# Attention of batches 3 to 7 at other steps, and another order in the prologue, in an attention and mixture-of-experts kernel

## The chip, the core and the metric

The kernel runs on one core of one Trainium2 chip. The metric is the device time of one execution in microseconds (us). The core has five engines with a queue each: TensorE (PE; its weight loads are PEld), VectorE (DVE), ScalarE (ACT), GpSimd (POOL) and SyncE (SP), which here issues the DMAs.

## The reference

For each of 8 batches and 8 heads, 576 tokens with 64 features are first gathered into 32 memory slots by a softmax of phi, each token then attends to the slots, and the result, 4608 rows of 512, goes through four experts whose outputs are summed with the given probabilities:

```python
a = np.exp(phi - np.max(phi, axis=2, keepdims=True))
a = a / (np.sum(a, axis=2, keepdims=True) + 1e-09)
k_m = np.einsum('bhsm,bhsd->bhmd', a, k)
v_m = np.einsum('bhsm,bhsd->bhmd', a, v)
attn = softmax(1.0 / np.sqrt(64) * np.matmul(q, k_m.transpose(0, 1, 3, 2)))
x = rows_of(np.matmul(attn, v_m))            # 4608 x 512
p = domain_probs / (domain_probs.sum(-1, keepdims=True) + 1e-09)
for e in range(4):
    out += p[:, e:e + 1] * (np.maximum(x @ w1[e], 0.0) @ w2[e])
```

## The kernel before

**Numbers in two parts.** A float32 factor is held as a rounded part ("high", cast by ScalarE) and the remainder ("low", input minus high, by VectorE or GpSimd). A product takes three matmuls: high x high, high x low, low x high. So nearly every tile needs a cast and a subtraction: of weights in `split` (L142, L143), of keys and values in `kv_split` (L266, L267), of h in `first` (L565, L567).

**The steps.** Batches go in four pairs. x @ w1 is not formed through x: the attention weights of a batch (AT, transposed) are multiplied by vw, the product of v_m and w1. `first(s)` makes one 128-row block of h for a half of a batch (six matmuls of 256 or 320 columns, L553 to L555; L565 and L567 empty the bank), `second(s)` multiplies such a block with w2 (six or nine matmuls of 512 columns, L583 to L585), summing in PSUM over 8 steps, after which `accumulate` (L603, L605) weighs the sums by the expert's probability into acc. There are 512 steps: 128 per pair (PAIR), 32 per expert (STEPS), 16 per batch, 8 per half. One step runs `accumulate` when sums have ended, then the work that the plan holds for it, then `first(s + 2)` and `second(s)`.

**The products vw.** `vw_mm` multiplies v of two batches with a block of w1 (L453 to L455); `vw_out` (L473, L474) empties it: for each of the two batches a cast of 64x512 on ScalarE and a subtraction on VectorE, both from PSUM. For the pairs and experts that concern us `vw_steps` puts the matmuls at a step and the emptying into the next. Emptying stands in steps 51, 52, 59 to 64; 115, 116, 123 to 128; 147, 148, 155 to 160; 179, 180, 187 to 192.

**Attention in the plan.** The table ATT has a row for each of the batches 2 to 7: a start step, the steps of the scores' matmuls, and the steps of the transposes. `attention(b, s, scores, turns)` puts the parts at fixed distances from the start s: `load_phi` at s; the maxima `phi_max` (L192, two per batch) at s + 3; the exponentials `phi_exp` (L201) at s + 4; the norms `phi_norm` (L206 to L209) at s + 5 and s + 6; transposes of the weights (tpa, L223) and their emptying into a (L231, L232) from s + 7; for each of four head pairs hp a `kv_split` at s + 10 + 3 hp, matmuls (L278, into x) two steps later, their copy xs (`kv_out`, L289) one after that; `kv_fold` (kvp) at s + 18 and s + 24 with `kv_pick` (L311, L312) a step later; `v_hi` at s + 26 and `write_vs` (vs, L367 to L370) at s + 27. Scores are made by `scores_mm` and, in the three following steps, `scores_max` (L393, L396), `scores_exp` (L402) and `soft` (L409 to L412).

**PSUM.** Four banks ("pm") go round for h's sums, products, x, kvp, scores and transposes, and four ("p2") for the second product. A matmul that takes a bank waits until the last user's emptying is done.

**Order.** From step 36 (FREE) on, instructions run on each engine in the order of the program; before that a scheduler orders them, except for the prologue, written out by hand (L755 to L839): batch 0's attention, its four products, the first weights. `keep_warm` issues matmuls on an identity tile. Remainders of the first w1 block are made by GpSimd but for one by VectorE; the first w2 block is cast there by ScalarE, and its remainders made by VectorE in L836. Products 0 and 2 go through `vw_out_by_copy`: two ScalarE copies, and a GpSimd subtraction (L482) from the SBUF copy. Loads of inputs go into `stage` tiles (L128) and are issued in the order in which the plan takes them; a load waits for its buffer.

Of the kernel before, what the change touches and what calls it, by code (L numbers as in the profile page):

```python
# [31 lines left out]
F32 = mybir.dt.float32  # L32
F32R = mybir.dt.float32r
# [8 lines left out]
P = 128  # L42
# [10 lines left out]
STAGE = 4  # L53
# [19 lines left out]
PAIR_AT = ((18, 19, 26, 27), (28, 29, 30, 31))  # L73

ATT = {
    2: (22, (92, 96, 100), (97, 101, 104)),
    3: (42, (104, 107, 110), (112, 113, 114)),
    4: (PAIR, (PAIR + 40, PAIR + 44, PAIR + 48), (PAIR + 45, PAIR + 49, PAIR + 53)),
    5: (PAIR + 22, (PAIR + 76, PAIR + 80, PAIR + 84), (PAIR + 112, PAIR + 113, PAIR + 114)),
    6: (PAIR + 44, (2 * PAIR + 24, 2 * PAIR + 28, 2 * PAIR + 32), (2 * PAIR + 29, 2 * PAIR + 33, 2 * PAIR + 37)),  # L80
    7: (PAIR + 66, (2 * PAIR + 98, 2 * PAIR + 102, 2 * PAIR + 106), (2 * PAIR + 112, 2 * PAIR + 113, 2 * PAIR + 114)),
}

UNITS_1 = (1, 5, 5, 6, 5, 6, 8, 9, 10, 11, 11, 12, 17, 13, 13, 20)
# [7 lines left out]
def body(ctx: ExitStack, tc: tile.TileContext, qm, qt, kv, kvt, phi, prob, w1, w1d, w2, out):  # L92
# [16 lines left out]
        kind, *i = key  # L109
        return {"kv": kv, "kvt": kvt, "qm": qm, "qt": qt, "w1": w1, "w1d": w1d, "w2": w2}[kind][tuple(i)]  # L110

    order, staged, count = [], {}, [0, 0]

    def stage_ahead(upto):
        while count[0] < min(upto, len(order)):
            i, src = count[0], source(order[count[0]])
            if STAGE <= i < STAGE + 4:
                t = work.tile([P, 1024], F32, name="stage", tag="acc", bufs=4)
            else:
                t = work.tile([P, 1024], F32, name="stage", tag="stage", bufs=STAGE)  # L120
            n = 1
            for d in src.shape[1:]:
                n *= d
            names = "abcd"[:len(src.shape) - 1]
            t = t[:, :n].rearrange(
                f"p ({' '.join(names)}) -> p {' '.join(names)}", **dict(zip(names, src.shape[1:]))
            )
            nc.sync.dma_start(t, src)  # L128
            staged[i] = t
            count[0] += 1  # L130
# [170 lines left out]
    def kv_pick(b, g):  # L301
        if g == 0:
            st["v", b] = att.tile([P, NP, M], F32, name="v", tag="v", bufs=2)
        for w in range(2):
            for i in range(2):
                r, m = slice(64 * i, 64 * i + 64), slice(M * i, M * i + M)
                lo = slice(2 * M + M * i, 2 * M + M * i + M)
                a = slice(2 * g, 2 * g + 2)
                dst = st["v", b][r, a] if w else kT[b % 4][r, a, m]
                src = st["kvp", b, g][r, :, w]  # L310
                (nc.vector.tensor_copy if i and b == 0 else nc.scalar.copy)(dst, src[:, :, m])  # L311
                nc.vector.tensor_add(dst, dst, src[:, :, lo])  # L312

    def unit_kv(b, hp):
        def emit(raw):
# [157 lines left out]
            nc.scalar.copy(t[r, 0, :], ps[r])  # L473
            nc.vector.tensor_sub(t[r, 1, :], ps[r], t[r, 0, :].bitcast(F32))  # L474

    def vw_out_by_copy(ps, fh, hp):
        g, r = hp // 2, slice(64 * (hp % 2), 64 * (hp % 2) + 64)
        t = vw_tile(0, 0, 0, fh, g)
        tmp = att.tile([P, 2, 512], F32, name="vwc", tag="vw1", bufs=5)
        nc.scalar.copy(tmp[r, 0, :], ps[r])  # L480
        nc.scalar.copy(t[r, 0, :], ps[r])
        nc.gpsimd.tensor_sub(t[r, 1, :], tmp[r, 0, :], t[r, 0, :].bitcast(F32))  # L482
# [157 lines left out]
    for fh in range(2):  # L640
        for g in range(2):
            at(W1_1[2 * fh + g], unit_w1(0, 0, fh, g))
            for i in range(2):
                vw_at(VW_1[4 * fh + 2 * g + i], 0, 0, fh, 2 * g + i, (1,))
    def attention(b, s, scores, turns):

        at(s, lambda: load_phi(b))
        for g in range(2):
            at(s + 3, lambda g=g: phi_max(b, g))
            at(s + 4, lambda g=g: phi_exp(b, g))  # L650
            at(s + 5 + g, lambda g=g: phi_norm(b, g))
            at(s + 7 + g, lambda g=g: phi_turn(b, g))
            at(s + 8 + g, lambda g=g: phi_turn_out(b, g))
        at(s + 9, lambda: phi_turn_tail(b))
        at(s + 9, unit_tail(b))
        at(s + 10, lambda: phi_turn_tail_out(b))
        for hp in range(NP):
            def load(raw, hp=hp):
                for c2 in range(2):
                    kv_split(b, hp, raw, c2, nc.gpsimd)  # L660
            def multiply(hp=hp):
                for c2 in range(2):
                    kv_mm(b, hp, c2)
                kv_mm_tail(b, hp)
            at(s + 10 + 3 * hp, (("kv", b, hp), load))
            at(s + 12 + 3 * hp, multiply)
            at(s + 13 + 3 * hp, lambda hp=hp: kv_out(b, hp))
        for g in range(2):
            at(s + 18 + 6 * g, lambda g=g: [kv_fold(b, 2 * g + i) for i in range(2)])
            at(s + 19 + 6 * g, lambda g=g: kv_pick(b, g))  # L670
        def write():
            if b < 4:
                write_vt(b)
        at(s + 26, lambda: (v_hi(b), write()))
        at(s + 27, lambda: write_vs(b))
        for t0, n in zip((0, 2, 4), scores):
            at(n, (q_key(b, t0), lambda q, t0=t0: scores_mm(b, t0, q)))
            at(n + 1, lambda t0=t0: scores_max(b, t0))
            at(n + 2, lambda t0=t0: scores_exp(b, t0))
            at(n + 3, lambda t0=t0: soft(b, t0))  # L680
        for t0, n in zip((0, 2, 4), turns):
            at(n, lambda t0=t0: transposes(b, t0))
            at(n + 1, lambda t0=t0: transposes_out(b, t0))
# [72 lines left out]
    with tc.manual_schedule():  # L756
        raw = {key: take(later) for later, key in enumerate(early)}
        stage_ahead(len(early) + 4)
        nc.scalar.copy(att.tile([P, 1], F32, name="woken", tag="woken"), ident[:, :1])
        nc.sync.dma_start(pt, prob)  # L760
        keep_warm(10)
        dve, gps = nc.vector, nc.gpsimd
        for g in range(2):
            phi_max(0, g)
        for g in range(2):
            phi_exp(0, g)
        kvr = lambda hp: raw["kv", 0, hp]
# [24 lines left out]
        for hp in (2, 3):
            for c2 in range(2):
                kv_mm(0, hp, c2)
            kv_mm_tail(0, hp)
            if hp == 2:
                for i in range(2):
                    kv_fold(0, i)
        keep_warm(3)
        kv_pick(0, 0)  # L800
        w1g = [raw["w1", 0, 0, g] for g in range(2)]
        split_w1(w1g[0], 0, 0, gps)
        for hp in (2, 3):
            kv_out(0, hp)
        write_vt(0, slice(0, 1))
        q = raw["qm", 0, 0]
        scores_mm(0, 0, q, (0, 1))
        for hp in (2, 3):
            kv_fold(0, hp)
        keep_warm(5)  # L810
        kv_pick(0, 1)
        scores_mm(0, 0, q, (2, 3))
        split_w1(w1g[0], 0, 1, dve)
        write_vt(0, slice(1, 2))
        keep_warm(2)
        split_w1(w1g[1], 0, 2, gps)
        split_w1(w1g[1], 0, 3, gps)
        for i in range(2):
            t = wp.tile([P, 2, DM], F32R, name="w2", tag="w2", bufs=NJ + 1)
            nc.scalar.copy(t[:, 0, :], raw["w2", 0, 0][:, i, :])  # L820
            w2t[0, 0, i] = t
        scores_max(0, 0)
        scores_exp(0, 0)
        pv = [vw_mm(0, 0, hp, ("p2", 4)) for hp in range(4)]
        vw_out_by_copy(pv[0], 0, 0)
        vw_out_by_copy(pv[2], 0, 2)
        soft(0, 0)
        keep_warm(6)
        vw_out(pv[1], 0, 0, 0, 1, (0,))
        transposes(0, 0)  # L830
        transposes_out(0, 0)
        keep_warm(4)
        vw_out(pv[3], 0, 0, 0, 3, (0,))
        for i in range(2):
            t = w2t[0, 0, i]
            dve.tensor_sub(t[:, 1, :], raw["w2", 0, 0][:, i, :], t[:, 0, :].bitcast(F32))  # L836
        for s in range(AHEAD):
            first(s)
        probabilities()  # L839
# [53 lines left out]
```

## Time and profile before

| | us |
|---|---|
| median of three runs | 1423.62 (1422.99 to 1423.77) |
| the profiled execution | 1424.37 |
| its span, first to last instruction | 1422.6 |
| TensorE busy in the span | 1396.9 (98%) |
| VectorE busy | 653.1 (46%) |
| ScalarE busy | 568.6 (40%) |
| GpSimd busy | 395.3 (28%) |

The mean granted TensorE clock is 0.996 of full. A row of the timeline gives the start of an instruction in us from the span's start, its duration, the engine, the line, output <- input, and in brackets the idle time before it with what ended it. Matmul ends are modelled: the row of a matmul is longer than the distance to the next one. A row "xN" holds N instructions that follow one another.

### The profile page before, as it was taken

How to read it: one execution, taken by the hardware profiler on the slowest of the kernel's cores; microseconds unless marked ns; L12 is line 12 of the kernel's file. 1: busy time of each engine (PE TensorE's matmuls, PEld its weight loads, DVE VectorE, ACT ScalarE, POOL GpSimd, SP SyncE). 2: the span in 40 equal slices, each digit the busy share in tenths (PEclk: the TensorE clock that was granted, in tenths of full speed). 3: DMA queues.
4: the chain of work that ended last, by engine and by line, in shares of the span. 5: the costliest groups of instructions: out<-in, count | busy, mean ns of one | idle time of the engine just before them, and what ended most of it. 6: DMA issues, size and time to landing. Idle time of an engine off the chain costs nothing.

```text
span 1422.6 us, 21651 instructions
## 1 busy us (share of the span) xinstructions
PE 1396.9 (98%) x7748; PEld 1217.2 (86%) x7748; DVE 653.1 (46%) x1565; ACT 568.6 (40%) x1524; POOL 395.3 (28%) x315
## 2 busy tenths in 40 slices
PE   7999999999999989999999999999999999999998
PEld 7788888888888878888888888888888888888887
DVE  7885454535553546454443345434343322223222
ACT  7655455533354454553353443534332312122221
POOL 4300244412234162433342433424220202020200
PEclk9999999999999999999999999999999999999999
DMA  5632322684233143234468676786841623333201
GB/s 202 209 108 90 106 74 92 225 255 132 75 128 95 56 132 97 72 109 140 131 230 269 228 270 185 260 229 217 256 139 45 186 75 104 75 104 75 60 31 37
DMA packets 62843, 199.16 MB, mean 140 GB/s; under 512 B 10384, under 2 KB 11536, under 8 KB 62736
## 3 DMA queue, kind: packets, MB, share of 16 engines
q1 hardware_dynamic: 62736, 197.77, 44.4%
q8 instruction: 62, 1.02, 0.3%
q14 instruction: 45, 0.37, 0.1%
HBM read 146.35 MB, written 51.38 MB: 139 GB/s over the span
## 4 chain that ended last, share of the span: by engine, by line
PE 91%; DVE 4%; ACT 3%; DMA 1%; issue 1%; POOL 0%; SPq 0%; ACTq 0%; DVEq 0%
PE p L585 18%; PE p L584 17%; PE p L583 17%; PE p L553 9%; PE p L555 9%; PE p L554 9%; PE pv L506 3%; PE x L278 2%; PE sc L383 2%; DVE vw L474 1%; ACT vw L473 1%; ACT w L142 1%; PE tp L433 1%; PE pv L453 1%; DMA stage<-in_w 1%
## 5 line engine op out<-in xcount | busy, mean ns | idle before, releaser
L143 POOL TENSOR_TENSOR w<-stage,w 128x512 fp32r<-128x512 f32 x227 | 293.2, 1294 | 734.0 <-ACT w L142 710.4
L567 DVE SCALAR_TENSOR_TENSOR h<-p,h 128x256 fp32r<-128x256 f32 x512 | 215.5, 421 | 440.7 <-ACT h L565 303.0
L585 PE MATMUL p<-w,h 128*128 128x512 f32 x1024 | 402.7, 394 | 1.0 <-DVE nm L195 1.0
L584 PE MATMUL p<-w,h 128*128 128x512 f32 x1024 | 401.4, 392 | 0.4 <-DVE w L143 0.4
L583 PE MATMUL p<-w,h 128*128 128x512 f32 x1024 | 401.8, 393 | 0.0
L565 ACT ACTIVATE h<-p 128x256 fp32r<-128x256 f32 x512 | 196.6, 385 | 482.7 <-PE p L555 464.2
L553 PE MATMUL p<-AT,vw 128*128 128x256 f32 (+1 forms) x1024 | 307.8, 301 | 8.5 <-DVE vw L474 3.1
L555 PE MATMUL p<-AT,vw 128*128 128x256 f32 (+1 forms) x1024 | 302.5, 296 | 0.1
L554 PE MATMUL p<-AT,vw 128*128 128x256 f32 (+1 forms) x1024 | 301.8, 295 | 0.7 <-DVE AT L445 0.7
L585 PEld LDWEIGHTS p<-w,h 128*128 128x128 f32 x1024 | 192.3, 188 | 43.9 <-DVE nm L195 1.5
L553 PEld LDWEIGHTS p<-AT,vw 128*128 128x128 f32 x1024 | 192.7, 188 | 30.3 <-ACT xs L289 3.7
L584 PEld LDWEIGHTS p<-w,h 128*128 128x128 f32 x1024 | 192.5, 188 | 23.1 <-DVE w L143 0.8
L583 PEld LDWEIGHTS p<-w,h 128*128 128x128 f32 x1024 | 192.6, 188 | 22.6 <-ACT h L565 0.3
L554 PEld LDWEIGHTS p<-AT,vw 128*128 128x128 f32 x1024 | 192.8, 188 | 20.2 <-DVE AT L445 0.9
L555 PEld LDWEIGHTS p<-AT,vw 128*128 128x128 f32 x1024 | 192.4, 188 | 0.4 <-issue 0.3
L142 ACT CAST w<-stage 128x512 fp32r<-128x512 f32 x262 | 161.1, 618 | 7.3 <-DMA stage<-in_w 5.0
L567 DVE SCALAR_TENSOR_TENSOR hm<-p,hm 128x64 fp32r<-128x64 f32 x256 | 56.1, 219 | 139.0 <-ACT h L565 137.5
L565 ACT ACTIVATE hm<-p 128x64 fp32r<-128x64 f32 x256 | 57.0, 223 | 153.1 <-PE p L555 153.0
L509 DVE TENSOR_TENSOR vst<-pv,vst 128x512 fp32r<-128x512 f32 x80 | 55.3, 692 | 111.4 <-ACT vst L508 111.1
L267 POOL TENSOR_TENSOR kvs<-stage,kvs 128x512 fp32r<-128x512 f32 x58 | 75.0, 1314 | 98.9 <-ACT kvs L266 98.0
L508 ACT CAST vst<-pv 128x512 fp32r<-128x512 f32 x80 | 47.0, 587 | 121.9 <-PE pv L506 120.5
L474 DVE TENSOR_TENSOR vw<-pv,vw 64x512 fp32r<-64x512 f32 x94 | 64.4, 688 | 29.6 <-ACT vw L473 28.1
(95 smaller groups left out, 1174.0 us busy)
## 6 DMA issues: line engine op xcount, KB each, us to landing
stage<-in_w SPq DMA_DIRECT2D x92, 512.0 KB, 4.0
vwd<-vst SPq DMA_DIRECT2D x80, 512.0 KB, 3.5
vw<-vwd SPq DMA_DIRECT2D x320, 128.0 KB, 4.0
stage<-in_w1d SPq DMA_DIRECT2D x40, 512.0 KB, 3.8
stage<-in_kv SPq DMA_DIRECT2D x32, 512.0 KB, 3.8
stage<-in_qm SPq DMA_DIRECT2D x16, 512.0 KB, 4.2
out<-acc SPq DMA_DIRECT2D x32, 256.0 KB, 2.1
ph<-in_phi SPq DMA_DIRECT2D x16, 288.0 KB, 4.2
```

The source lines that it names most:

```text
L142: nc.scalar.copy(dst[:, 0, :], raw)
L143: eng.tensor_sub(dst[:, 1, :], raw, dst[:, 0, :].bitcast(F32))
L267: eng.tensor_sub(t[:, 1], src, t[:, 0].bitcast(F32))
L474: nc.vector.tensor_sub(t[r, 1, :], ps[r], t[r, 0, :].bitcast(F32))
L553: nc.tensor.matmul(ps, w[:, 0, f], at_t[:, g, 0, c], start=g == 0, stop=False)
L554: nc.tensor.matmul(ps, w[:, 0, f], at_t[:, g, 1, c], start=False, stop=False)
L555: nc.tensor.matmul(ps, w[:, 1, f], at_t[:, g, 0, c], start=False, stop=g == 1)
L565: nc.scalar.activation(t[:, 0, to], ps[:, at_], AF.Relu)
L567: nc.vector.scalar_tensor_tensor(t[:, 1, to], ps[:, at_], 0.0, t[:, 0, to].bitcast(F32), ALU.max, ALU.subtract)
L583: nc.tensor.matmul(po[t], x[:, 0, :], w[:, 0, :], start=j == 0, stop=False)
L584: nc.tensor.matmul(po[t], x[:, 0, :], w[:, 1, :], start=False, stop=False)
L585: nc.tensor.matmul(po[t], x[:, 1, :], w[:, 0, :], start=False, stop=j == NJ - 1)
```

## The change

ATT gets one more column, the step at which `v_hi` and `write_vs` stand (before: start + 26). Batch 2 stays. Batch 3 starts 4 steps earlier. Batch 4 keeps its start, is written 9 steps later, and its scores and transposes stand 6 to 8 steps earlier. Batch 5 starts 4 steps later, batches 6 and 7 start 4 steps earlier. `kv_pick` issues its four copies and then its four adds, where a copy and an add alternated. In the prologue `vw_out_by_copy` is gone: all four products are emptied by `vw_out`. GpSimd makes the remainder of one more w1 block and of both w2 blocks (now by `split_w2`), three `keep_warm` matmuls less are issued ahead of the transposes and four stand behind them instead of behind their emptying. Two more loads get a buffer of their own at the start, in a tile of the kind AT. Lines after the table shift by 5 to 10.

```diff
 ATT = {
-    3: (42, (104, 107, 110), (112, 113, 114)),
-    5: (PAIR + 22, (PAIR + 76, PAIR + 80, PAIR + 84), (PAIR + 112, PAIR + 113, PAIR + 114)),
+    3: (38, 65, (104, 107, 110), (112, 113, 114)),
+    5: (PAIR + 26, PAIR + 53, (PAIR + 76, PAIR + 80, PAIR + 84), (PAIR + 112, PAIR + 113, PAIR + 114)),
 ...
-            if STAGE <= i < STAGE + 4:
+            if STAGE + 4 <= i < STAGE + 6:
+                if i == STAGE + 4:
+                    spare.append(att.tile([P, 2 * 2 * S], F32, name="stage", tag="AT", bufs=3))
+                t = spare[0][:, 1024 * (i - STAGE - 4):1024 * (i - STAGE - 3)]
+            elif STAGE <= i < STAGE + 4:
 ...
-                (nc.vector.tensor_copy if i and b == 0 else nc.scalar.copy)(dst, src[:, :, m])
-                nc.vector.tensor_add(dst, dst, src[:, :, lo])
+                parts.append((dst, src[:, :, m], src[:, :, lo]))
+        for n, (dst, hi, _) in enumerate(parts):
+            (nc.vector.tensor_copy if n == 1 and b == 0 else nc.scalar.copy)(dst, hi)
+        for dst, _, lo in parts:
+            nc.vector.tensor_add(dst, dst, lo)
 ...
-        at(s + 26, lambda: (v_hi(b), write()))
-        at(s + 27, lambda: write_vs(b))
+        at(written, lambda: (v_hi(b), write()))
+        at(written + 1, lambda: write_vs(b))
 ...
-        split_w1(w1g[0], 0, 1, dve)
+        split_w1(w1g[0], 0, 1, gps)
 ...
-        for i in range(2):
-            t = wp.tile([P, 2, DM], F32R, name="w2", tag="w2", bufs=NJ + 1)
-            nc.scalar.copy(t[:, 0, :], raw["w2", 0, 0][:, i, :])
-            w2t[0, 0, i] = t
         scores_max(0, 0)
+        pv = [vw_mm(0, 0, hp, ("p2", 4)) for hp in range(4)]
+        vw_out(pv[0], 0, 0, 0, 0, (0,))
         scores_exp(0, 0)
-        pv = [vw_mm(0, 0, hp, ("p2", 4)) for hp in range(4)]
-        vw_out_by_copy(pv[0], 0, 0)
-        vw_out_by_copy(pv[2], 0, 2)
         soft(0, 0)
-        keep_warm(6)
-        vw_out(pv[1], 0, 0, 0, 1, (0,))
+        keep_warm(3)
+        for hp in (1, 2):
+            vw_out(pv[hp], 0, 0, 0, hp, (0,))
         transposes(0, 0)
+        keep_warm(4)
         transposes_out(0, 0)
-        keep_warm(4)
         vw_out(pv[3], 0, 0, 0, 3, (0,))
         for i in range(2):
-            t = w2t[0, 0, i]
-            dve.tensor_sub(t[:, 1, :], raw["w2", 0, 0][:, i, :], t[:, 0, :].bitcast(F32))
+            split_w2(0, 0, i, raw["w2", 0, 0], gps)
```

VectorE's queue at the end of the prologue, before, from the softmax sum of batch 0's first scores to h of step 0 (h_401). The numbers tell tiles apart; w1_458 and w1_461 are blocks of the next half of w1:

```order
L409 TENSOR_REDUCE z_363<-at_334 128x16
L410 TENSOR_SCALAR z_363<-z_363 128x16
L411 RECIPROCAL z_363<-z_363 128x16
L412 TENSOR_TENSOR at_334<-at_334,z_363 128x512
L474 TENSOR_TENSOR vw_353<-pv_341,vw_353 64x512
L143 TENSOR_TENSOR w1_458<-stage_115,w1_458 128x512
L445 TENSOR_TENSOR AT_377<-tp_378,AT_377 128x2x256
L474 TENSOR_TENSOR vw_358<-pv_349,vw_358 64x512
L836 TENSOR_TENSOR w2_328<-stage_111,w2_328 128x512
L836 TENSOR_TENSOR w2_330<-stage_111,w2_330 128x512
L567 SCALAR_TENSOR_TENSOR h_401<-p1_394,h_401 128x256
```

The same place after (h of step 0 is h_393, the blocks of the next half of w1 are w1_450, w1_453, w1_458):

```order
L148 TENSOR_TENSOR w1_450<-stage_114,w1_450 128x512
L418 TENSOR_REDUCE z_351<-at_329 128x16
L419 TENSOR_SCALAR z_351<-z_351 128x16
L420 RECIPROCAL z_351<-z_351 128x16
L421 TENSOR_TENSOR at_329<-at_329,z_351 128x512
L483 TENSOR_TENSOR vw_347<-pv_335,vw_347 64x512
L483 TENSOR_TENSOR vw_362<-pv_339,vw_362 64x512
L454 TENSOR_TENSOR AT_365<-tp_366,AT_365 128x2x256
L483 TENSOR_TENSOR vw_362<-pv_343,vw_362 64x512
L148 TENSOR_TENSOR w1_453<-stage_114,w1_453 128x512
L148 TENSOR_TENSOR w1_458<-stage_116,w1_458 128x512
L568 SCALAR_TENSOR_TENSOR h_393<-p1_386,h_393 128x256
```

One remainder of the next w1 half now stands ahead of the softmax sum and two ahead of h, four product remainders (L483; three of them in these rows) come from PSUM where two did, and both of w2 are gone.

GpSimd at the same place, before:

```order
L143 TENSOR_TENSOR w1_264<-stage_107,w1_264 128x512
L143 TENSOR_TENSOR w1_322<-stage_109,w1_322 128x512
L143 TENSOR_TENSOR w1_325<-stage_109,w1_325 128x512
L482 TENSOR_TENSOR vw_353<-vwc_354,vw_353 64x512
L482 TENSOR_TENSOR vw_358<-vwc_359,vw_358 64x512
L253 TENSOR_TENSOR tl_642<-stage_480,tl_642 64x512 x2
```

and after:

```order
L148 TENSOR_TENSOR w1_263<-stage_107,w1_263 128x512
L148 TENSOR_TENSOR w1_307<-stage_107,w1_307 128x512
L148 TENSOR_TENSOR w1_321<-stage_109,w1_321 128x512
L148 TENSOR_TENSOR w1_324<-stage_109,w1_324 128x512
L148 TENSOR_TENSOR w2_380<-stage_111,w2_380 128x512
L148 TENSOR_TENSOR w2_383<-stage_111,w2_383 128x512
L258 TENSOR_TENSOR tl_634<-stage_472,tl_634 64x512 x2
```

The two product remainders went, and one of w1 and two of w2 came.

VectorE around steps 155 and 156, before (vs is batch 4's, zs and ph are batch 5's, vw the product remainders):

```order
L474 TENSOR_TENSOR vw<-pv,vw 64x512 x2
L370 TENSOR_TENSOR vs<-v,vh 64x2x32
L369 CAST vs<-vh 64x2x32
L370 TENSOR_TENSOR vs<-v,vh 64x2x32 x2
L369 CAST vs<-vh 64x2x32
L370 TENSOR_TENSOR vs<-v,vh 64x2x32
L206 TENSOR_SCALAR zs<-zs 128x1
L207 RECIPROCAL zs<-zs 128x1
L208 TENSOR_SCALAR ph<-ph,zs 128x576
L209 COPY ph<-ph 128x64
L567 SCALAR_TENSOR_TENSOR h<-p_5208,h 128x256
L474 TENSOR_TENSOR vw<-pv,vw 64x512 x2
```

and after, steps 157 to 159:

```order
L483 TENSOR_TENSOR vw<-pv,vw 64x512 x2
L197 TENSOR_REDUCE nm<-ph 128x1
L200 TENSOR_SCALAR nm<-nm 128x1
L197 TENSOR_REDUCE nm<-ph 128x1
L200 TENSOR_SCALAR nm<-nm 128x1
L568 SCALAR_TENSOR_TENSOR h<-p_5239,h 128x256
L483 TENSOR_TENSOR vw<-pv,vw 64x512 x2
L568 SCALAR_TENSOR_TENSOR h<-p_5270,h 128x256
L483 TENSOR_TENSOR vw<-pv,vw 64x512 x2
L211 TENSOR_SCALAR zs<-zs 128x1
L212 RECIPROCAL zs<-zs 128x1
L213 TENSOR_SCALAR ph<-ph,zs 128x576
```

Batch 4's vs has left, batch 5's maxima (nm) stand in step 157, and its first norm follows in 159.

VectorE in steps 175 and 176, before, up to the second acc (hm and h are h's remainders, nm is batch 6's):

```order
L312 TENSOR_TENSOR kT_78<-kT_78,kvp 64x2x32 x2
L312 TENSOR_TENSOR v<-v,kvp 64x64 x2
L192 TENSOR_REDUCE nm<-ph 128x1
L195 TENSOR_SCALAR nm<-nm 128x1
L192 TENSOR_REDUCE nm<-ph 128x1
L195 TENSOR_SCALAR nm<-nm 128x1
L567 SCALAR_TENSOR_TENSOR hm<-p_5843,hm 128x64
L567 SCALAR_TENSOR_TENSOR h<-p_5843,h 128x256
L605 SCALAR_TENSOR_TENSOR acc<-p_5622,pt,acc 128x512
L605 SCALAR_TENSOR_TENSOR acc<-p_5626,pt,acc 128x512
```

and after, steps 174 to 176:

```order
L568 SCALAR_TENSOR_TENSOR hm<-p_5830,hm 128x64
L568 SCALAR_TENSOR_TENSOR h<-p_5830,h 128x256
L568 SCALAR_TENSOR_TENSOR hm<-p_5867,hm 128x64
L568 SCALAR_TENSOR_TENSOR h<-p_5867,h 128x256
L606 SCALAR_TENSOR_TENSOR acc<-p_5621,pt,acc 128x512
L606 SCALAR_TENSOR_TENSOR acc<-p_5625,pt,acc 128x512
L237 TENSOR_TENSOR a<-tpa,a 128x2x4x64
```

The adds of `kv_pick` and the maxima no longer stand ahead of acc.

## Rows read from the trace of the kernel before

**Rows 1.** The page: busy share, and the share of the chain by engine.
```profile
PE 1396.9 (98%) x7748; PEld 1217.2 (86%) x7748; DVE 653.1 (46%) x1565; ACT 568.6 (40%) x1524; POOL 395.3 (28%) x315
...
PE 91%; DVE 4%; ACT 3%; DMA 1%; issue 1%; POOL 0%; SPq 0%; ACTq 0%; DVEq 0%
```

**Rows 2.** Busy time by stretch: length, PE, PEld, DVE, ACT, POOL, clock, DMA share, GB/s.
```profile
0.00:45.00 45.00, 37.75 (x224) 33.18 (x225) 35.42 (x81) 29.41 (x69) 16.13 (x21) 0.92 0.60 218
...
380.00:425.00 45.00, 45.00 (x246) 39.01 (x245) 23.10 (x46) 21.87 (x49) 14.53 (x12) 1.00 0.30 98
...
480.00:520.00 40.00, 34.23 (x181) 28.16 (x180) 26.13 (x53) 21.16 (x50) 14.74 (x12) 0.96 0.19 57
...
550.00:620.00 70.00, 66.19 (x375) 56.55 (x374) 40.67 (x99) 37.48 (x96) 28.68 (x23) 1.00 0.30 93
620.00:900.00 280.00, 280.00 (x1567) 245.60 (x1566) 128.09 (x304) 114.28 (x310) 96.10 (x75) 1.00 0.63 199
```

**Rows 3.** TensorE's waits, whole span: total, times, longest.
```profile
PE p L553 <- DVE vw L474: 3.1, 4, 1.4
...
PE p L553 <- DVE h L567: 2.4, 2, 2.3
PE p L553 <- ACT xs L289: 2.3, 2, 1.2
...
PE p L583 <- DVE acc L605: 2.0, 2, 1.5
```

**Rows 4.** Timeline, VectorE at step 47, TensorE at step 61.
```profile
186.80 1.22 DVE L209 COPY ph<-ph 128x64 f32<-128x64 f32 x1
...
231.98 0.39 PE L553 MATMUL p<-AT,vw 128*128 128x256 f32 x1 [1.18 <-ACT xs L289]
```

**Rows 5.** Timeline of TensorE, steps 154 to 159.
```profile
490.34 0.28 PE L553 MATMUL p<-AT,vw 128*128 128x256 f32 x1
...
493.13 0.28 PE L553 MATMUL p<-AT,vw 128*128 128x256 f32 x1
...
500.75 0.39 PE L553 MATMUL p<-AT,vw 128*128 128x256 f32 x1 [2.25 <-DVE h L567]
...
502.22 0.63 PE L585 MATMUL p<-w,h 128*128 128x512 f32 x1
...
510.25 0.36 PE L553 MATMUL p<-AT,vw 128*128 128x256 f32 x1 [1.38 <-DVE vw L474]
```

**Rows 6.** Timeline of VectorE and TensorE, steps 175 and 176.
```profile
559.52 0.75 DVE L192 TENSOR_REDUCE nm<-ph 128x1 f32<-128x576 f32 x1
560.31 0.15 DVE L195 TENSOR_SCALAR nm<-nm 128x1 f32<-128x1 f32 x1
...
560.73 0.40 PE L585 MATMUL p<-w,h 128*128 128x512 f32 x1
562.61 0.50 PE L583 MATMUL p<-w,hm 128*128 128x512 f32 x1 [1.49 <-DVE acc L605]
```

**Rows 7.** Timeline of TensorE, steps 187 to 190.
```profile
608.29 0.36 PE L553 MATMUL p<-AT,vw 128*128 128x256 f32 x1 [1.11 <-DVE vw L474]
...
612.49 0.38 PE L553 MATMUL p<-AT,vw 128*128 128x256 f32 x1 [1.17 <-ACT xs L289]
```

**Rows 8.** Timeline of VectorE, steps 156 to 158.
```profile
498.02 1.18 DVE L208 TENSOR_SCALAR ph<-ph,zs 128x576 f32<-128x576 f32 x1
...
503.46 0.69 DVE L474 TENSOR_TENSOR vw<-pv,vw 64x512 fp32r<-64x512 f32 x1 [0.37 <-ACT vw L473]
504.80 0.68 DVE L474 TENSOR_TENSOR vw<-pv,vw 64x512 fp32r<-64x512 f32 x1 [0.65 <-ACT vw L473]
```

**Rows 9.** Timeline of ScalarE, step 154: one exponential.
```profile
487.07 0.78 ACT L201 ACTIVATE ph<-ph,nm 128x576 f32<-128x576 f32 x1 [0.67 <-DVE nm L195]
487.75 0.19 ACT L201 ACTIVATION_READ_ACCUMULATOR ph<-ph,nm 128x1 f32 x1
```

**Rows 10.** Timeline of VectorE and TensorE at the end of the prologue.
```profile
28.00 1.59 DVE L412 TENSOR_TENSOR at<-at,z 128x512 f32<-128x512 f32 x1
...
31.30 0.69 DVE L445 TENSOR_TENSOR AT<-tp,AT 128x512 fp32r<-128x512 f32 x1
...
34.94 0.40 PE L585 MATMUL p<-w,h 128*128 128x512 f32 x1
```

More of the change, by code (lines that the diff above doesn't have):

```diff
@@ L75 @@
 ATT = {
-    2: (22, (92, 96, 100), (97, 101, 104)),
-    3: (42, (104, 107, 110), (112, 113, 114)),
-    4: (PAIR, (PAIR + 40, PAIR + 44, PAIR + 48), (PAIR + 45, PAIR + 49, PAIR + 53)),
-    5: (PAIR + 22, (PAIR + 76, PAIR + 80, PAIR + 84), (PAIR + 112, PAIR + 113, PAIR + 114)),
-    6: (PAIR + 44, (2 * PAIR + 24, 2 * PAIR + 28, 2 * PAIR + 32), (2 * PAIR + 29, 2 * PAIR + 33, 2 * PAIR + 37)),
-    7: (PAIR + 66, (2 * PAIR + 98, 2 * PAIR + 102, 2 * PAIR + 106), (2 * PAIR + 112, 2 * PAIR + 113, 2 * PAIR + 114)),
+    2: (22, 48, (92, 96, 100), (97, 101, 104)),
+    3: (38, 65, (104, 107, 110), (112, 113, 114)),
+    4: (PAIR, PAIR + 35, (PAIR + 34, PAIR + 37, PAIR + 41), (PAIR + 38, PAIR + 42, PAIR + 45)),
+    5: (PAIR + 26, PAIR + 53, (PAIR + 76, PAIR + 80, PAIR + 84), (PAIR + 112, PAIR + 113, PAIR + 114)),
+    6: (PAIR + 40, PAIR + 67, (2 * PAIR + 24, 2 * PAIR + 28, 2 * PAIR + 32), (2 * PAIR + 29, 2 * PAIR + 33, 2 * PAIR + 37)),
+    7: (PAIR + 62, PAIR + 88, (2 * PAIR + 98, 2 * PAIR + 102, 2 * PAIR + 106), (2 * PAIR + 112, 2 * PAIR + 113, 2 * PAIR + 114)),
 }
@@ L110, in source @@
         return {"kv": kv, "kvt": kvt, "qm": qm, "qt": qt, "w1": w1, "w1d": w1d, "w2": w2}[kind][tuple(i)]
-    order, staged, count = [], {}, [0, 0]
+    order, staged, count, spare = [], {}, [0, 0], []
     def stage_ahead(upto):
@@ L303, in kv_pick @@
             st["v", b] = att.tile([P, NP, M], F32, name="v", tag="v", bufs=2)
+        parts = []
         for w in range(2):
@@ L474, in vw_out @@
             nc.vector.tensor_sub(t[r, 1, :], ps[r], t[r, 0, :].bitcast(F32))
[L476 to L482, printed above, removed]
     def vw_unit(k, e, fh, hp, odds, tag):
@@ L644, in body, with attention @@
                 vw_at(VW_1[4 * fh + 2 * g + i], 0, 0, fh, 2 * g + i, (1,))
-    def attention(b, s, scores, turns):
+    def attention(b, s, written, scores, turns):
         at(s, lambda: load_phi(b))
```

## The prediction

> **What bounds the kernel now.** First the page's shares: TensorE is busy in 98% of the span, and the chain that ended last is TensorE for 91% of it, VectorE 4%, ScalarE 3% [rows 1]. Only TensorE's idle time can be won. The table by stretches says where it is [rows 2]: 7.25 us in the first 45, 5.77 between 480 and 520, 3.81 between 550 and 620, nothing between 380 and 425 or 620 and 900. The list of waits names the releasers [rows 3]: the remainder of a product (vw L474), of h (L567), xs (L289), acc (L605). All is VectorE or ScalarE work that came late while both are under half busy, so the order is what decides, not the load.
>
> A wait shows less than it costs: a 512-column matmul lasts 0.40, but the next one starts 0.23 later. L585 at 560.73 and L583 at 562.61 [rows 6] are 1.88 apart, so the 1.49 shown cost 1.65. I count so throughout.
>
> Lost before, from step 36 on:
> - A, steps 48 to 62: xs 1.18 shown at 231.98 [rows 4], 1.33; acc, 0.5 as the lesser of the two in the list (2.0 less 1.5 [rows 3]), 0.64; three small ones, 1.1. Sum 3.1.
> - C, steps 155 to 162: an undisturbed step with a product takes 2.79 (first L553 at 490.34 and 493.13 [rows 5]). From 493.13 to 510.25 there are three, 8.4, and some 0.5 of transposes; 17.1 passed, so 8.2 went. Of this 1.6 is the clock: after the wait of 2.25 at 500.75 eight 512-column rows lasted about 0.63, not 0.40 [rows 5], the level of 1.2 GHz. With 0.9 in two waits at 517, C is 9.1.
> - D: 1.65 in step 176 [rows 6]; 1.11 and 1.17 shown in steps 189 and 190, 1.28 and 1.33 [rows 7]. Sum 4.3.
> - 0.2 at step 146.
> In all 16.7.
>
> **The change part by part.** *C.* Evicting one product for two batches is a chain ScalarE, VectorE, ScalarE, VectorE; its two L474 start 1.34 apart (503.46 and 504.80 [rows 8]), so 2.7 per step against TensorE's 2.79. There is no room: further work on these two engines lands on TensorE, less what the rotating PSUM banks keep in store. Before, steps 155 to 158 had batch 4's vs and batch 5's first norm on VectorE (491.6 to 495.2, 3.6), its second norm (497.6 to 500.4, 2.7; L208 took 1.18 there beside a POOL remainder [rows 8]) and two pairs of a copies (0.58 and 0.67 each, 2.5): 8.8. Lost were 7.5 without the clock, so the store is about 1.3. After, vs has gone to step 164; batch 5, started at 154 instead of 150, has there its two maxima in step 157 (0.75 + 0.15 each [rows 6], 1.8), two exponentials in 158 (0.78 + 0.19 each [rows 9], 1.9) and two norms in 159 and 160 (undisturbed 1.03 each, 2.1); its a copies come later. Sum 5.8, less 1.3: 4.5. Bounds: with the exponentials hidden beside VectorE's part of the chain 2.6; with both norms stretched by POOL as before (1.6 each) 7.7, and with the clock falling again 9.3. I take 4.5, the undisturbed rows. Gain 4.6.
>
> *D.* Batch 6 starts at 168 instead of 172. Its maxima stood in step 175 (0.75 each, from 559.52 [rows 6]), so that L605 of step 176 came late, and with it the bank that L583 needs. Now they are in 171, and nothing but h stands before L605; next late would be h, which has a step in hand: 1.65 won. In steps 187 to 191 xs was behind evictions in 188 and 191; now it is behind those of 187 and 190, with kv_pick in 187: four copies and then four adds, 0.2 each, so 0.8 on either engine, and xs 0.37. With the eviction's 2.7 that is over 2.79 by about 1.1; 0.5 more for step 190. So 1.6 of 2.6 stays. Gain 1.65 + 1.0 = 2.65; bounds 1.0 and 4.
>
> *A.* Batch 3 starts at 38 instead of 42: its norms leave steps 47 and 48, where L209, a copy of 0.20 elsewhere, took 1.22 [rows 4] ahead of L605. The acc wait goes, and most of the small ones. The multiplications move to steps 50 to 59, all clear of evictions but the last, whose xs is still in step 60 beside one. I leave 1.0 of 3.1. Gain 2.1; bounds 0.5 and 3.
>
> kv_pick alone: a term of its own only where it stands beside evictions, counted above.
>
> *Prologue.* L482 (2.94 for two on GpSimd) and its copies go; VectorE reads PSUM for all four products, 0.69 more for each of two. L412 took 1.59 beside L482 [rows 10], and 0.69 undisturbed: 0.9 won. Against it the order puts a w1 remainder (0.68, about 1.0 behind GpSimd's own) ahead of the softmax sum, which eats it. AT's remainder, at 31.30 [rows 10], comes about 0.2 earlier. Then the two w2 remainders run on GpSimd, about 32 to 35, and two w1 remainders of VectorE stand ahead of step 0's h; each waits for the POOL operation's end as L412 did. h's remainder ends near 36.3 instead of 34.5, and L585, at 34.94 before [rows 10], waits some 1.6. But those w1 remainders stood behind h before (35.7 to 37.0) and are then done: VectorE's next lateness, three waits of 0.4 to 1.0 up to 56, shrinks by about what was paid (1.3), and the loads that no longer wait for L836 take 0.3. Net 0. Bounds: 1.0 won (the 0.9 kept), 2.5 lost (1.6 and one more blocked operation, nothing back).
>
> Batch 7, the later scores and turns lie where TensorE has no idle time before [rows 2]: nothing; if the cover went, one step's softmax of 1.8 on VectorE.
>
> Sum 4.6 + 2.65 + 2.1 + 0 = 9.4. The profiled execution took 1424.37 (span 1422.6, 1.8 around it), 0.75 over the median 1423.62: 1424.37 - 9.4 - 0.75 = 1414.2.
>
> **A rule that speaks against it.** L412, L208 and L209 read and write SBUF only, and took 1.59, 1.18 and 1.22 when they started inside a POOL operation; L445, which reads PSUM, kept its 0.69 [rows 4, 8, 10]. The Trainium skill, "SBUF — State Buffer", section "Who interferes with whom", says that a VectorE instruction with two SBUF inputs contends with a GpSimd instruction that reads SBUF, that whichever is issued first holds the shared port pair for its whole length, and that the other fully blocks; for L412 the trace agrees. By that rule alone the remainders given to GpSimd cost the prologue 2.5 and the sum is 1416.7; without it the prologue wins 1.0 and the sum is 1413.2.
>
> **Rivals.** 1, *C stays*: both norms meet POOL work, the clock falls again (C 9.3), the prologue loses 2.5. Gain 16.7 - (1.0 + 0.2 + 9.3 + 1.6) - 2.5 = 2.1: 1421.5 (with a neutral prologue 1419.0). For: 5.8 of work is still in the stretch. Against: it is split over four steps, 1.8 to 2.1 in each but one.
> 2, *slower, by blocked VectorE operations*: each that starts inside a POOL operation ahead of a TensorE wait costs 0.9 (L412). From eleven of them the 9.4 is gone, from fourteen the kernel is measurably slower. Five stand in the prologue, a dozen in the moved norms and vs. Sixteen cost 14.4: 1428.6. The rule above is its ground. Against: before, with all its POOL work, only four or five such operations preceded a wait.
> 3, *more goes*: the stretch 380 to 425 has the same evictions and no idle [rows 2]. If 155 to 162 becomes like it (C 1.0, A 0.3, D 0.3, prologue 1.0 won): 16.7 - 1.8 + 1.0 = 15.9: 1407.7. Against: that stretch has little attention beside it.
> 4, *the stall only moves*: 2.7 plus a cast of 0.6 is over 2.79 wherever attention stands, and the change does not do what its table says: 1423.6. Against: 380 to 425 again.
>
> **How the numbers follow.** Forecast 0.55 (own range 1410 to 1418.5), rival 1 0.14, rival 2 0.05, rival 3 0.20, rival 4 0.06. The low end 1406 takes in most of rival 3, the high end 1421.5 most of rival 1; about 0.2 is left out. A measurement of this kernel tells 0.2%, 2.85 us, from no change, so faster is below 1420.8: 0.55 + 0.20 + 0.08 of rival 1 = 0.83. Same: 0.06 of rival 1 and 0.05 of rival 4, 0.11. Slower 0.06.
>
> **What would show it.** In the list of waits acc falls from 2.0 to under 0.3 and xs from 2.3 to about 1; between 480 and 520 TensorE idles some 3 us less than 5.77. Around step 0 TensorE waits 1 to 2 us for h. L412's counterpart takes 0.7. The prediction is wrong if the stretch of steps 155 to 162 still loses 8 or more, if new waits of over 2 us stand at 163 to 174, where batch 4's scores now are, or if the first 60 us become longer by over 2.5.

## The result: slower by 3.2 us, and the profile after

The changed kernel takes 1427.03 us (median of ten, 1426.36 to 1428.86) against 1423.88 of before in the same rounds: ratio 1.0023, interval 1.0013 to 1.0033. Forecast were 1414.2 and 0.83 for faster. The profiled execution took 1426.93 and has a span of 1425.1, 2.5 more than before. Two slow executions, one of f3 (1520.52) and one of g1 (2200.47), are left out of the medians below.

The page of the changed kernel: busy shares, and the chain by engine.

```profile
PE 1397.7 (98%) x7742; PEld 1218.4 (85%) x7742; DVE 663.7 (47%) x1562; ACT 568.3 (40%) x1524; POOL 396.0 (28%) x316
...
PE 90%; DVE 6%; ACT 2%; issue 1%; DMA 1%; SPq 0%; ACTq 0%; DVEq 0%
```

VectorE is busy 10.6 longer with three instructions less, and its share of the chain rose from 4% to 6% [rows 1]. So operations got longer. The first four of TensorE's waits after step 3 (total, times, longest):

```profile
PE p L586 <- DVE h L568: 3.3, 1, 3.3
PE tpa L228 <- DVE ph L213: 2.4, 2, 1.6
PE p L554 <- DVE vw L483: 1.8, 3, 1.0
PE x L283 <- DVE a L251: 1.6, 1, 1.6
```

Against [rows 3] the acc wait is gone, as forecast, and xs has left the wait for L553; the waits of 3.3, 2.4 and 1.6 are at new places. By stretch (columns as in [rows 2]):

```profile
150.00:300.00 150.00, 145.09 (x796) 127.11 (x795) 76.75 (x184) 70.69 (x194) 58.70 (x46) 0.99 0.39 129
...
480.00:520.00 40.00, 35.78 (x200) 30.33 (x199) 24.42 (x46) 17.80 (x41) 10.41 (x8) 0.96 0.17 57
520.00:550.00 30.00, 29.17 (x170) 25.44 (x170) 20.52 (x43) 14.15 (x39) 12.70 (x10) 0.94 0.42 137
550.00:620.00 70.00, 68.93 (x395) 60.13 (x394) 37.08 (x93) 38.59 (x106) 31.47 (x25) 1.00 0.31 102
```

TensorE now idles 4.91 between 150 and 300, where it was 2.27. Three places of the timeline tell why. The first is step 65, batch 3's write (GpSimd, VectorE, and the TensorE row that waits):

```profile
243.98 5.01 POOL L148 TENSOR_TENSOR w<-stage,w 128x512 fp32r<-128x512 f32 x4 [2.64 <-ACT w L147]
...
244.19 1.14 DVE L363 CAST vt<-vh 64x64 fp32r<-64x64 f32 x1
245.25 1.37 DVE L364 TENSOR_TENSOR vt<-v,vh 64x64 fp32r<-64x64 f32 x1
246.63 1.18 DVE L363 CAST vt<-vh 64x64 fp32r<-64x64 f32 x1
247.74 1.33 DVE L364 TENSOR_TENSOR vt<-v,vh 64x64 fp32r<-64x64 f32 x1
249.08 0.19 DVE L363 CAST vt<-vh 64x64 fp32r<-64x64 f32 x1
249.19 0.22 DVE L364 TENSOR_TENSOR vt<-v,vh 64x64 fp32r<-64x64 f32 x1
...
250.25 0.50 PE L586 MATMUL p<-w,h 128*128 128x512 f32 x1 [3.31 <-DVE h L568]
```

The same operation takes 0.19 alone and 1.14 beside GpSimd. The four long ones end at 245.33, 246.62, 247.82 and 249.07, each 0.05 to 0.08 after one of GpSimd's four (245.28, 246.54, 247.77, 248.99): each VectorE operation waits for the remainder that is running. From 249.08 on VectorE runs at its own pace. TensorE lost 3.5 here and 1.6 more because its clock fell after the wait: the 512-column rows from 250.98 on start 0.43 apart, the 1.2 GHz level, and the granted clock between 250.3 and 254.0 is 0.54. The four are the last of the eight w2 remainders that belong to steps 61 to 68; before, this write stood at 68, beside the last alone, and one operation was long:

```profile
250.69 1.19 DVE L354 CAST vt<-vh 64x64 fp32r<-64x64 f32 x1 [0.28 <-ACT vh L338]
251.80 0.21 DVE L355 TENSOR_TENSOR vt<-v,vh 64x64 fp32r<-64x64 f32 x1
```

The second is batch 2's write in step 48, which did not move; batch 3's keys, which come four steps earlier, and the weight remainders around them came onto it. The first row is from before, where this write met no GpSimd work, the others are from after:

```profile
189.91 0.19 DVE L354 CAST vt<-vh 64x64 fp32r<-64x64 f32 x1
...
190.00 2.54 POOL L272 TENSOR_TENSOR kvs<-stage,kvs 128x512 fp32r<-128x512 f32 x2
...
190.02 1.35 DVE L364 TENSOR_TENSOR vt<-v,vh 64x64 fp32r<-64x64 f32 x1
...
195.14 1.20 PE L283 MATMUL x<-kvs,a 128*128 128x256 f32 x8 [1.61 <-DVE a L251]
```

The third is batch 5's two norms, in steps 159 and 160:

```profile
509.22 1.26 POOL L148 TENSOR_TENSOR w<-stage,w 128x512 fp32r<-128x512 f32 x1 [1.44 <-ACT w L147]
...
509.36 1.44 DVE L213 TENSOR_SCALAR ph<-ph,zs 128x576 f32<-128x576 f32 x1
510.83 0.20 DVE L214 COPY ph<-ph 128x64 f32<-128x64 f32 x1
...
515.15 1.44 DVE L213 TENSOR_SCALAR ph<-ph,zs 128x576 f32<-128x576 f32 x1
516.62 1.14 DVE L214 COPY ph<-ph 128x64 f32<-128x64 f32 x1
```

The transposes of these norms make TensorE wait 1.57 and 1.22. Batch 7's first norm is a smaller case of the same:

```profile
624.38 2.75 POOL L148 TENSOR_TENSOR w<-stage,w 128x512 fp32r<-128x512 f32 x2 [2.24 <-ACT w L147]
...
624.54 1.44 DVE L213 TENSOR_SCALAR ph<-ph,zs 128x576 f32<-128x576 f32 x1
```

The prologue went nearly as told: L412's counterpart takes 0.69, and the wait for h of step 0 is 1.60.

```profile
28.77 0.69 DVE L421 TENSOR_TENSOR at<-at,z 128x512 f32<-128x512 f32 x1
...
32.28 3.38 DVE L148 TENSOR_TENSOR w<-stage,w 128x512 fp32r<-128x512 f32 x2
...
36.17 0.50 PE L586 MATMUL p<-w,h 128*128 128x512 f32 x1 [1.60 <-DVE h L568]
```

Set side by side by the start of each step (the first L553 matmul in it, L554 after), the changed kernel is 0.8 ahead at step 36, 2.6 behind at 72, 3.0 at 154, 1.2 at 240, and 2.6 at 505. The last 1.4 come without any wait, over 265 steps in which both programs do the same work; they are called the drift below.

### The profile page after: what moved, and what is told of

It is laid out like the page before. It is cut to its first block, busy times and chain, and to the rows that moved or that the text cites. A ratio compares the mean times of both kernels' runs of the same rounds, so it can differ in the third digit from the quotient of the medians.

```text
span 1425.1 us, 21643 instructions
## 1 busy us (share of the span) xinstructions
PE 1397.7 (98%) x7742; PEld 1218.4 (85%) x7742; DVE 663.7 (47%) x1562; ACT 568.3 (40%) x1524; POOL 396.0 (28%) x316
## 4 chain that ended last, share of the span: by engine, by line
PE 90%; DVE 6%; ACT 2%; issue 1%; DMA 1%; SPq 0%; ACTq 0%; DVEq 0%
PE p L586 18%; PE p L584 17%; PE p L585 17%; PE p L554 9%; PE p L555 9%; PE p L556 9%; PE pv L507 3%; PE sc L392 2%; PE x L283 2%; DVE vw L483 1%; ACT vw L482 1%; PE pv L462 1%; PE pv L464 1%; PE pv L463 1%; DVE vt L364 1%
## 5 line engine op out<-in xcount | busy, mean ns | idle before, releaser
L148 POOL TENSOR_TENSOR w<-stage,w 128x512 fp32r<-128x512 f32 x230 | 297.5, 1297 | 752.7 <-ACT w L147 727.8
L554 PE MATMUL p<-AT,vw 128*128 128x256 f32 (+1 forms) x1024 | 309.1, 302 | 1.9 <-DVE vw L483 1.8
L554 PEld LDWEIGHTS p<-AT,vw 128*128 128x128 f32 x1024 | 193.1, 189 | 23.1 <-PE pv L464 2.5
L483 DVE TENSOR_TENSOR vw<-pv,vw 64x512 fp32r<-64x512 f32 x96 | 65.7, 687 | 29.8 <-ACT vw L482 28.1
```

What stands on the lines that cost most here:

```text
L148: eng.tensor_sub(dst[:, 1, :], raw, dst[:, 0, :].bitcast(F32))
L554: nc.tensor.matmul(ps, w[:, 0, f], at_t[:, g, 0, c], start=g == 0, stop=False)
```

## The experiments

Theory A: VectorE's operations that read SBUF were moved beside GpSimd's remainders and wait for them. B: the chain of product evictions is the bound, and a stall only moves. C: VectorE's own queue is too long. D, for the drift: addresses.

**e1 and e2: the two writes alone.**

```diff
-    3: (38, 65, (104, 107, 110), (112, 113, 114)),
+    3: (38, 69, (104, 107, 110), (112, 113, 114)),
```

> The changed kernel with one number other: batch 3's v_hi and write_vt at step 69 instead of 65, write_vs at 70. Theory A (VectorE's small operations stood inside GpSimd's four w2 remainders): the vt operations take 0.19 to 0.22 each instead of 1.14 to 1.37, the wait of 3.3 for h's remainder at 247 goes, and with it the low clock behind it, 5.1 in all: 1422 (1421 to 1423). Theory B (the stall only moves): another wait of 2 or more comes in steps 63 to 72, 1425 to 1427.

Measured 1421.55, ratio to before 0.9985 (0.9976 to 0.9993): 5.5 less than the changed kernel. e2 puts batch 2's number from 48 to 55 too.

> As the run before, and batch 2 written at step 55 instead of 48 as well. Theory A: batch 2's vt operations (1.21 to 1.35 each at 188.84, beside batch 3's tail and key remainders, which came four steps earlier) take 0.2, the wait of 1.61 for a's last part in step 49 goes: 1.8 less than the run before, 1420.4 (1419.5 to 1421.5). Theory B: no change against the run before.

Measured 1419.49, ratio 0.9971 (0.9959 to 0.9982). In e2's trace TensorE has no idle time between 150 and 300, and VectorE runs through batch 3's write:

```profile
150.00:300.00 150.00, 150.00 (x828) 131.91 (x828) 71.28 (x188) 72.65 (x200) 60.27 (x47) 1.00 0.42 144
```

```profile
246.88 0.19 DVE L363 CAST vt<-vh 64x64 fp32r<-64x64 f32 x1
246.99 0.22 DVE L364 TENSOR_TENSOR vt<-v,vh 64x64 fp32r<-64x64 f32 x1
```

No wait took the place of those removed: B falls for this stretch. Two numbers in the table cost 7.5.

**e3 and e4: table and prologue apart.** e3 is the kernel before with the new ATT, the column `written` and the new kv_pick; e4 the changed kernel with the old steps:

```diff
-    3: (38, 65, (104, 107, 110), (112, 113, 114)),
+    3: (42, 68, (104, 107, 110), (112, 113, 114)),
 ...
```

> The kernel before with the new table of attention steps and the new order in kv_pick alone; prologue and loads as before. Theory A: the table loses 2.4 by itself between steps 36 and 100 (3.5 more lost there than before) and wins about 2 in steps 155 to 200, so this is about as before plus 2 to 4: 1426 to 1428; the prologue's part is then within 1. Rival: the prologue is what made it slower, and this is at or under 1421.

Measured 1425.61, ratio 1.0013 (1.0004 to 1.0021), 0.4 under the expected range.

> The changed kernel with the steps of the table as before: only the prologue, the two early loads and kv_pick's order are changed. From the two traces the start of step 20 is 0.7 earlier and that of step 36 0.8: 1423.9 - 0.8 = 1423.1 (1422 to 1424.5). Rival (the prologue lost 1.8 in the wait for h): 1425 to 1426.5.

Measured 1424.08, ratio 1.0002 (0.9993 to 1.0011): no change, in the expected range. In its trace step 36 starts 1.3 earlier than before, and more than half of that is gone at step 505.

**e5: GpSimd's remainders taken out of the two places.**

```diff
+        if (k, e) in ((0, 2), (1, 1)):
+            def high(raw, j):
+                t = wp.tile([P, 2, DM], F32R, name="w2", tag="w2", bufs=NJ + 1)
+                nc.scalar.copy(t[:, 0, :], raw[:, j % 2, :])
+                nc.gpsimd.memset(t[:, 1, :].bitcast(F32), 0.0)
+                w2t[k, e, j] = t
```

> The changed kernel, with GpSimd's remainders of w2 left out for expert 2 of the first pair and expert 1 of the second (cast in steps 61 to 68 and 157 to 164) and a memset of zeros by GpSimd in the place of each: those products lack their low part of w2. Theory A (what blocks is a GpSimd operation that reads SBUF while VectorE reads SBUF): batch 3's vt operations at 244 to 249 take about 0.2 or little more, L213 and L214 at 509 to 518 about 0.52 and 0.20, the waits at 247 and 511 shrink by 3 and 1: 1427 - 5.1 - 2.5 = 1419.5 (1418 to 1421.5). Theory C (VectorE is late for another reason, its own queue): the durations stay, 1426 to 1428. If only the operations with two inputs recover and the casts keep over 1, 1423 to 1425.

Measured 1416.54, ratio 0.9952 (0.9935 to 0.9968), 1.5 under the expected range, with the changed table untouched. The write at step 65, and the first norm in the stretch:

```profile
244.23 0.19 DVE L373 CAST vt<-vh 64x64 fp32r<-64x64 f32 x1
244.34 0.21 DVE L374 TENSOR_TENSOR vt<-v,vh 64x64 fp32r<-64x64 f32 x1
...
504.26 0.52 DVE L223 TENSOR_SCALAR ph<-ph,zs 128x576 f32<-128x576 f32 x1
504.81 0.20 DVE L224 COPY ph<-ph 128x64 f32<-128x64 f32 x1
```

VectorE has the same queue and the same order, and these operations have their own length. C falls. Between steps 154 and 200 this run goes 6.75 ahead of the kernel before, the changed kernel 0.95: the blocking cost 5.8 there, more than the 2.5 expected, part of it the low clock at 520, which went too. What is left of the loss in steps 155 to 166 is 8.8 - 5.8 = 3.0. Of it 1.2 is a wait of batch 4's first scores in step 162: they start at 508.93, right after a product remainder that ends at 508.83, which points to the evictions for this part. The memsets (16 of 0.53) waited for no cast, and none ran beside the operations named, so whether GpSimd's writing alone would block is not shown.

**e6: the norms put where GpSimd is idle.** On e2:

```diff
-    4: (PAIR, PAIR + 35, ...
-    5: (PAIR + 26, PAIR + 53, ...
-    7: (PAIR + 62, PAIR + 88, ...
+    4: (PAIR, PAIR + 38, ...
+    5: (PAIR + 18, PAIR + 53, ...
+    7: (PAIR + 64, PAIR + 91, ...
```

> As e2 (batch 2 written at 55, batch 3 at 69), and batch 4 written at 166, batch 5 started at 146 so that its norms stand in steps 151 and 152 and its exponentials in 150, ahead of the product evictions and of GpSimd's w2 remainders; batch 7 started at 192. Theory A: steps 155 to 166 lose under 2 instead of 8.8, batch 7's wait at 628 (1.0) goes: 1420.4 - 7 - 1 = 1412.5 (1410.5 to 1415). Theory B (the evictions with any attention beside them are the bound): 1417 to 1420.

Measured 1411.84, ratio 0.9917 (0.9902 to 0.9931). TensorE idles 1.1 between 480 and 520, where [rows 2] had 5.77, and both norms run free:

```profile
480.00:520.00 40.00, 38.86 (x242) 34.28 (x241) 21.04 (x40) 24.97 (x57) 25.02 (x20) 1.00 0.37 122
```

```profile
474.25 0.52 DVE L213 TENSOR_SCALAR ph<-ph,zs 128x576 f32<-128x576 f32 x1
474.80 0.20 DVE L214 COPY ph<-ph 128x64 f32<-128x64 f32 x1
```

The evictions are the same and still in steps 155 to 160, with batch 5's keys on GpSimd beside them, so B in its full form falls here too. But the maxima and exponentials left the evictions together with the norms, so e6 by itself does not tell what the block was worth; e5, which left all of them there, does.

**f1 to f4: the drift.** The early loads' tile is the first of the kind AT, and tiles get addresses in the order of their kinds: AT stands at byte 124096 of a partition instead of 181856, vw at 151904 instead of 124256; the other tiles that lay between vw and AT's old place move by the same 27648 bytes as vw. f1 takes the loads out of the changed kernel, f2 gives the kernel before one unused AT tile at that place:

```diff
-            if STAGE + 4 <= i < STAGE + 6:
 ...
-            elif STAGE <= i < STAGE + 4:
+            if STAGE <= i < STAGE + 4:
```

```diff
     load_phi(0)
+    att.tile([P, 2, 2, S], F32R, name="AT", tag="AT", bufs=3)
```

> The changed kernel without the two early loads into a spare AT buffer; that tile, allocated first, had also moved the AT and vw tiles to other addresses. Theory D (the addresses): between steps 240 and 505, where the two programs have the same work, the changed kernel drifts 1.40 behind the one before, in steps that repeat to within 1 ns, and 0.3 between 72 and 96; here that drift is 0, and the first 36 steps give back part of their 0.8: 1427.0 - 1.7 + 0.5 = 1425.8 (1424.8 to 1426.8). Rival: the drift comes from the rotation of PSUM banks or from fewer warm-up matmuls, and stays 1.4: 1427 to 1428.

> The kernel before with one AT tile allocated right after the first phi load and never used: AT and vw stand at the addresses of the changed kernel, nothing else differs. Theory D: a drift of 1.4 between steps 240 and 505 and as much again before: 1423.6 + 2 = 1425.6 (1425 to 1426.5). Rival: no drift, 1423.6.

f2 took 1425.79, ratio 1.0017 (1.0008 to 1.0026). First matmul of steps 240 and 505, in the kernel before and then in f2:

```profile
741.51 0.39 PE L553 MATMUL p<-AT,vw 128*128 128x320 f32 x1
...
1405.36 0.28 PE L553 MATMUL p<-AT,vw 128*128 128x256 f32 x1
```

```profile
743.32 0.39 PE L553 MATMUL p<-AT,vw 128*128 128x320 f32 x1
...
1408.57 0.28 PE L553 MATMUL p<-AT,vw 128*128 128x256 f32 x1
```

663.85 against 665.25, and the changed kernel needs the same 665.25. In f1 it is 663.85 again. Every kept trace with that tile shows 665.25 (the changed kernel, e1, e2, e4, e5, e6, f2), every one without it 663.85 (before, e3, f1, f3, f4, g1, g2). So D holds: the addresses alone, with not one instruction other, cost 1.4 in these steps and 1.6 in the medians of f2. f1 as a whole missed: 1429.37, ratio 1.0042 (1.0030 to 1.0054), 3.6 above the expected. Without the early loads its first 36 steps take 4.4 more than the changed kernel's. The queue of SyncE shows a load that comes late:

```profile
SPq L128 <- POOL w L143: 17.9, 1, 17.9
```

The load waits for the buffer from which GpSimd's late w2 remainders read, and later, in step 4, TensorE waits 2.99 for h. VectorE's rows ahead of that h show the block again, beside GpSimd's remainders of batch 1's keys:

```profile
51.50 1.77 DVE L143 TENSOR_TENSOR w<-stage,w 128x512 fp32r<-128x512 f32 x1
53.20 1.25 DVE L209 COPY ph<-ph 128x64 f32<-128x64 f32 x1
```

The first takes 0.67 to 0.68 undisturbed, the second 0.20. In f1 the clock fell after the wait as well (0.81 between 53 and 62). I had given these loads 0.5.

f3 takes the early loads out of e6 in the same way; f4 is f3 with

```diff
-            split_w2(0, 0, i, raw["w2", 0, 0], gps)
+            split_w2(0, 0, i, raw["w2", 0, 0], dve)
```

> The run with batch 5 at 146 (1411.84), without the two early loads and so with the addresses of before. Theory D: 1411.8 - 1.7 + 0.5 = 1410.6 (1409.6 to 1411.6). Rival: the loads were worth more than the addresses cost, 1412 to 1413.

> As the run before, with the two first w2 remainders on VectorE instead of GpSimd (as in the kernel before). The prediction's account of the prologue: TensorE's wait of 1.60 for h's remainder at 36.17 goes, and about as much comes back as later lateness, so step 20 starts within 0.5 of the run before: 1410.6 (1410 to 1411.2). Rival (the wait is paid in full): 1.5 less, 1409.1.

f3: 1414.87, ratio 0.9936 (0.9923 to 0.9949), above the expected; its drift is 0. Its times fall in two groups, 1412.1 to 1412.3 and 1414.9 to 1415.3, and the kept trace is of the first: it has the same block and the same wait of 3.0 in step 4 as f1, but its clock did not fall after it, and its first 36 steps take 2.4 more than e6's. f4: 1410.56, ratio 0.9911 (0.9898 to 0.9924). With w2's remainders back on VectorE step 36 starts 1.4 earlier than in f3's trace, so the time came out as expected by luck: f3, from which it was reckoned, had missed, and the wait was paid in full, as the rival had it.

**g1 and g2: the early loads without other addresses.** On e6; g2 has f4's line as well:

```diff
-                    spare.append(att.tile([P, 2 * 2 * S], F32, name="stage", tag="AT", bufs=3))
-                t = spare[0][:, 1024 * (i - STAGE - 4):1024 * (i - STAGE - 3)]
+                    wp.tile([P, 2, 512], F32R, name="w1", tag="w1", bufs=4)
+                t = wp.tile([P, 1024], F32, name="stage", tag="w2", bufs=NJ + 1)
```

> As the run with batch 5 at 146 (1411.84), with the two early loads in two w2 buffers instead of an AT buffer, so that AT, vw, w1 and w2 stand where they stood before. From the traces: that run starts step 36 1.2 earlier than the kernel before and drifts 1.7 later behind it; without the drift 1411.8 - 1.7 = 1410.1 (1409 to 1411.3), with no drift between steps 240 and 505. Rival (the loads' gain of 4.4 depended on the AT buffer): as the run without early loads, 1413 or more.

> As the run before, with the first two w2 remainders on VectorE. Without early loads this choice moved the start of step 36 by 1.44 (from 1.21 late to 0.23 early against the kernel before). Theory A: the wait of 1.60 for h goes and what it held back was held by VectorE alone, so 0.5 to 1 less: 1409.4 (1408.5 to 1410.5). Rival (with the loads early, GpSimd's remainders cost nothing that lasts): as the run before within 0.5.

g1: 1410.19, ratio 0.9900 (0.9884 to 0.9917), no drift: with f4 the fastest, some 14 under the kernel before in their rounds and over 16 under the changed one. g2: 1412.05, ratio 0.9911 (0.9895 to 0.9928), not the gain I expected: the wait for h at step 0 goes, but one of 3.0 comes in step 4, behind the same blocked operations as in f1 (1.76 and 1.25). g2 has the loads early, so late loads alone are not what makes this wait. The intervals of f4, g1 and g2 overlap; I don't rank them. Step 0's start also differs by over 1 us between traces with the same prologue (f1 and f3 by 1.3), so the prologue's terms under 1 are not settled.

## Why the prediction was wrong, step by step

- *A* was forecast to lose 1.0 and lost 6.9 (1.8 in step 49, 5.1 in 67 and 68). The step that failed is the one sentence "its norms leave steps 47 and 48": it followed batch 3's VectorE work out of the blocked place [rows 4] and followed neither its GpSimd work nor its write. Batch 3's tail, keys and the weight remainders beside them came onto batch 2's write, which the table leaves at 48, and the write at 65 went into w2's remainders. Both stood in the order of the two programs, and the price of a block in [rows 4, 8, 10]. e1 and e2 show both.
- *C* was forecast to lose 4.5 and lost 8.8, near its bound of 9.3: "I take 4.5, the undisturbed rows" was the wrong choice. GpSimd's work in steps 159 and 160 comes from the w2 casts of every step from 157 on, so a norm there had to meet it; the sum left it out and kept it for the upper bound. Of the 8.8, which runs to step 166, 1.0 is a wait of step 165 for batch 4's softmax; the scores and transposes moved there were costed at nothing. e5 shows the choice: with free norms the stretch loses 3.0, near the lower bound of 2.6.
- *D* held where it looked: acc's wait is gone and 1.5 is left at 186 and 187, forecast 1.6. Batch 7, costed at nothing because TensorE had no idle time there before, lost 1.2 in step 197, its norm blocked in the same way (L213 1.44). A place without waits says nothing of work that is new to it.
- *Prologue*: net 0 forecast, 0.8 ahead at step 36 and no change in e4. The wait of 1.6 was right to the digit; but without the loads, costed at 0.3, step 36 starts 1.2 (f3) to 3.6 (f1) later than before, so the loads are worth 2 to 4.4 beside GpSimd's late remainders and the rest costs the difference. The net was right by two errors.
- *Addresses*: 1.7 (1.4 from step 240 on, 0.3 between 72 and 96) that no view of the profile of before could show.

5.9 + 4.3 + 1.1 + 1.7, less 0.8, is 12.2; between the 1415.0 that the sum gave for a profiled execution and the 1426.9 of the one after lie 12.0.

Rival 2 was the mechanism, with a chance of 0.05: its ground was the block rule, told in a section of its own, and the sum then used that rule for the prologue and for C's upper bound only. Its price of 0.9 for a block was about right: the operations above took 0.9 to 1.2 more than alone. The rule of the Trainium skill ("SBUF — State Buffer", "Who interferes with whom") says that copies, casts and tensor_scalar operations can contend with GpSimd too, not only operations with two SBUF inputs; the casts at step 65 (1.14 instead of 0.19) and the norm's multiplication (1.44 instead of 0.52) agree with that. Against the rival was said that before "only four or five such operations preceded a wait"; but four in a row, 5.0 instead of 0.8, were more than the store (1.3 by the prediction's own account). One row of that section was misread: L445 at 31.30 kept its 0.69 with no GpSimd operation beside it, as L482 had ended at 30.71; L474 at 29.62, which also reads PSUM, took 0.69 inside L482 and is the fair comparison.

Most of the signs that the prediction gave for being wrong did not come, because they watched the places that it had costed: steps 155 to 162 lost about 7.7, no wait in 163 to 174 is over 1, and the first 60 us did not grow. One sign failed: between 480 and 520 TensorE idles 4.2, not some 3 less than 5.77.

## What to carry to other kernels

When a block of work is moved, list for every engine what it will stand beside, unmoved neighbours too, and write down for each small operation which long one of another engine runs at that time. An operation that is blocked ended here shortly after the other engine's, whatever its own length, so its row at an undisturbed place is a lower bound. Where one engine's work blocks another's, the free windows of the one are the places for the other: two numbers in a table were worth 7.5 here and four more 7.6.

## What the runs showed that was not expected

An allocation that no instruction uses made the kernel slower by 1.6 (f2, 1.0017, interval 1.0008 to 1.0026): AT, vw and smaller tiles at other SBUF addresses. It is no scatter: between steps 240 and 505 single steps are up to 20 ns shorter or 45 ns longer than before, and e4, f2 and the changed kernel agree in each to 1 ns. Which of the tiles matters, and why, wasn't tried.
